# Splitting the experts' weight chunks behind the attention on VectorE alone

## The chip, the cores and the metric

The kernel runs on one core of a Trainium2 chip. The metric is the device time of one execution in microseconds (us); the time before is the median of three runs.

Engines are named as in the profile: PE is TensorE (PEld its weight loads), ACT is ScalarE, DVE is VectorE, POOL is GpSimd, SP is SyncE, which issues most DMAs. Each engine runs its own instructions in the order in which they were written and waits for others by semaphores.

## What is computed

A gated linear attention over 4 x 768 tokens, then two mixture-of-experts layers, each with top-1 routing over 8 experts (model width 384, hidden width 1024). Cut to what matters:

```python
# attention, per batch and head
state = f[t][:, None] * state + outer(k[t], v[t]);  y[t] = q[t] @ state
# each of the two expert layers, on x of [3072, 384]
e = argmax(x @ w_gate);  gate = softmax(x @ w_gate)[e]
out[i] = gate[i] * (relu(x[i] @ w1[e]) @ w2[e])      # w1: 384 x 1024, w2: 1024 x 384
```

The first layer also has a capacity per expert.

## The kernel before

**Stages.** The attention runs over 24 tiles of 128 tokens and ends near 186 us. Then come 19 groups of rows (`G`): 9 of the first expert layer, 10 of the second. A group holds the rows of one expert (256 to 480 of them; an expert with two groups has a row count for each), gathered from DRAM by indirect DMAs that POOL issues (L295), one for each block of up to 128 rows.

**Products in two halves.** Each fp32 operand is held as a high part in the fast fp32r format and a low part, the remainder. A product is three matmuls: high by high, high by low, low by high. So every expert's weights are brought in as 12 raw chunks of 128 x 512 (6 of w1, 6 of w2), and each is split by `_split_chunk`: ACT copies the raw chunk to the high tile (L1025), then a vector engine subtracts it from the raw chunk to give the low tile (L1026). This subtraction, called **the split** below, has two inputs in SBUF and one output there, and nothing else in this kernel is done with it. Which engine takes it is decided at L1063 to L1069.

**A group on PE.** For each of 8 hidden blocks `fc`: `mm1` (L1163, 9 matmuls into a PSUM tile `hp`, of which there are two), on ACT the relu `hh` (L1174), on DVE the low part `hl` (L1175), and two blocks later `mm2` (L1187 to L1189, 9 matmuls). So PE's order is mm1(fc), mm2(fc-2), mm1(fc+1), mm2(fc-1), mm1(fc+2), and mm1(fc+2) needs the `hp` tile that hl(fc) has read last.

**What lies between.** A hand-written plan has 16 spots for a group, two for each fc: one between mm1 and the relu (even spots), one behind mm2 (odd spots). At spots 4 to 9 of the next group a finished group is turned back to rows (PE L926 or L1001, DVE `yr` L927 or L1002, two PSUM tiles shared with the next item); in the first layer also its routing runs there: a chain of small DVE operations (`choose`, L947 and L101 to L125) at spot 6 ends in the one-hot `oh` (L121, L123), which PE's ranking matmul at spot 7 (L131) waits for, then POOL's scatters (L273). In the second layer two small operations (`pw` L996, `td` L997) come ahead of the rows, and POOL scatters the result. At spots 12 and 13 the rows of the next group are turned (PE `tp` L1140, ACT `xh` L1148, DVE `xl` L1149), through the same two PSUM tiles. The 12 splits of the next expert are spread over the spots 0, 1, 2, 4, 5, 6, 8, 9, 10, 12, 13 and 14, and each stands behind what else the plan has at its spot; at an even spot that is ahead of hl on DVE. Single chains stand elsewhere: `flags` (L1287 its last but one) in the fifth group, `first2` with `_skip` (L869) in the eighth.

**The rule for the engine.** During the attention the 12 chunks of the first expert are split on GpSimd by name. Behind it no engine is named (`eng is None`): of the 12 chunks of an expert, those with `i % 3 == 2` went to DVE and the others to POOL, save for the second expert, of which 8 went to DVE and 4 to POOL. Of the 180 chunks behind the attention that makes 64 on DVE and 116 on POOL.

Of the kernel before, what the change touches and what calls it, by code (L numbers as in the profile page):

```python
# [1023 lines left out]
def _split_chunk(nc, hi, lo, raw, eng):  # L1024
    nc.scalar.copy(out=hi, in_=raw)  # L1025
    eng.tensor_tensor(out=lo, in0=raw, in1=hi.bitcast(F32), op=ALU.subtract)  # L1026


class _Weights:
# [23 lines left out]
    def split(self, eng=None):  # L1053
        i = self.done
        wi, c = divmod(i, 2 * NCH)
        k, q = divmod(c, NCH)
        pool = self.env.wp[wi % 2]
        if c == 0:
            self.t[wi] = {}
        if q == 0:  # L1060
            self.t[wi][k] = [
                pool.tile([P, NCC * FF], F32R, name=f"w{k}{u}_{wi}", tag=f"w{k}{u}") for u in "hl"
            ]  # L1063
        hi, lo = self.t[wi][k]
        s = slice(q * RAWC, (q + 1) * RAWC)
        if eng is None:

            eng = self.nc.vector if i % 3 == 2 or wi == 1 and i % 3 else self.nc.gpsimd
        _split_chunk(self.nc, hi[:, s], lo[:, s], self.raws.pop(i), eng)  # L1069
        self.done += 1  # L1070
        self.fetch()

# [729 lines left out]
```

## Time and profile before

| | us |
|---|---|
| median of 3 runs | 707.98 (705.53 to 710.4) |
| the profiled execution | 709.22 |
| its span, first to last instruction | 707.4 |
| PE busy, share of the span | 676.5, 96% |
| DVE busy | 409.8, 58% |
| POOL busy | 361.2, 51% |
| ACT busy | 322.2, 46% |
| mean granted TensorE clock | 0.991 |

An engine's idle time costs something only where PE, which is busy almost throughout, then waits. Ends of matmuls are modelled: a matmul is listed as busy until its result is out, while the next one starts earlier, so an idle time of PE is counted from that later end. "<-" in a row names what ended a wait. A row with "xN" is N instructions merged.

### The profile page before, as it was taken

The page shows a single profiled execution, that of the slowest core. Times are in us where ns is not written, and L with a number is a line of the kernel's source. Part 1 is how long each engine was busy: PE and PEld are TensorE (multiplying, and loading weights), DVE is VectorE, ACT ScalarE, POOL GpSimd, SP SyncE. Part 2 cuts the span into 40 slices and gives each one's busy share as a digit, 9 for nine tenths or more (in the row PEclk, how much of TensorE's full clock was granted, in tenths as well). Part 3 has the DMA queues.
Part 4 walks back from the last instruction along what each step waited for, and adds up shares of the span by engine and source line. Part 5 has one row for each costly group of instructions (what it writes and reads, how often), then busy time and mean ns, then how long its engine had stood idle before and what let it go on. Part 6 is the DMA issues. An engine that isn't in the chain of part 4 may idle for free.

```text
span 707.4 us, 15778 instructions
## 1 busy us (share of the span) xinstructions
PE 676.5 (96%) x5775; PEld 619.0 (87%) x5778; DVE 409.8 (58%) x1024; ACT 322.2 (46%) x697; POOL 361.2 (51%) x389
## 2 busy tenths in 40 slices
PE   7989999989999999999999899989999999999995
PEld 4878788877898989989999899989998899999994
DVE  4767777866486555745546654456344455464641
ACT  5668777743353434344343433144334334354420
POOL 5233444454365546565473651456656464576621
PEclk9999999999999999999999999999999999999998
DMA  8899899532485545355473520275445354454300
GB/s 191 248 203 224 199 183 215 127 83 93 131 258 159 152 120 155 97 154 141 126 185 97 159 95 1 68 237 161 141 115 164 101 155 131 136 154 147 92 25 20
DMA packets 63273, 99.79 MB, mean 141 GB/s; under 512 B 16588, under 2 KB 32942, under 8 KB 63187
## 3 DMA queue, kind: packets, MB, share of 16 engines
q1 hardware_dynamic: 55507, 83.06, 44.0%
q0 software_dynamic: 7680, 15.64, 7.9%
q8 instruction: 47, 0.77, 0.5%
q14 instruction: 39, 0.32, 0.2%
HBM read 82.90 MB, written 16.60 MB: 141 GB/s over the span
## 4 chain that ended last, share of the span: by engine, by line
PE 72%; DVE 9%; DMA 8%; issue 5%; ACT 2%; POOL 1%; SPq 0%; DVEq 0%; POOLq 0%; ACTq 0%
PE hpm L1163 27%; PE ypm L1187 8%; PE ypm L1188 8%; PE ypm L1189 8%; DMA out_dram<-yr,tdm 6%; PE y L509 3%; PE G L402 3%; PE sc L444 3%; PE tpm L1140 2%; PE kv L466 1%; PE tym L926 1%; PE warm L629 1%; PE tym L1001 1%; PE ltm L260 1%; PE kp L433 1%
## 5 line engine op out<-in xcount | busy, mean ns | idle before, releaser
L1174 ACT ACTIVATE hhm<-hpm 128x288 fp32r<-128x288 f32 (+11 forms) x152 | 72.4, 477 | 184.0 <-PE hpm L1163 163.5
L1163 PE MATMUL hpm<-xhm,w0h 128*128 128x288 f32 (+11 forms) x456 | 155.2, 341 | 0.4 <-DVE hlm L1175 0.3
L1187 PE MATMUL ypm<-hhm,w1h 128*128 128x288 f32 (+11 forms) x456 | 153.9, 338 | 0.0
L1175 DVE SCALAR_TENSOR_TENSOR hlm<-hpm,hhm 128x288 fp32r<-128x288 f32 (+11 forms) x152 | 81.2, 536 | 120.9 <-ACT hhm L1174 92.6
L1188 PE MATMUL ypm<-hlm,w1h 128*128 128x288 f32 (+11 forms) x456 | 150.6, 330 | 0.0
L1163 PE MATMUL hpm<-xhm,w0l 128*128 128x288 f32 (+11 forms) x456 | 150.5, 331 | 0.0
L1189 PE MATMUL ypm<-hhm,w1l 128*128 128x288 f32 (+11 forms) x456 | 150.4, 330 | 0.0
L1163 PE MATMUL hpm<-xlm,w0h 128*128 128x288 f32 (+11 forms) x456 | 144.6, 331 | 0.0
L1026 POOL TENSOR_TENSOR w0l<-raw,w0h 128x512 fp32r<-128x512 f32 x64 | 81.9, 1296 | 57.9 <-ACT w0h L1025 57.5
L1026 POOL TENSOR_TENSOR w1l<-raw,w1h 128x512 fp32r<-128x512 f32 x64 | 82.1, 1295 | 41.5 <-ACT w1h L1025 40.6
L295 POOL DMA_INDIRECT xrm<-x,idcm x64 | 69.8, 1090 | 55.6 <-DVE valm L1021 34.0
L1163 PEld LDWEIGHTS hpm<-xhm,w0h 128*128 128x128 f32 x456 | 86.3, 189 | 3.6 <-DVE hlm L1175 1.0
L1187 PEld LDWEIGHTS ypm<-hhm,w1h 128*128 128x128 f32 x456 | 85.9, 188 | 2.8 <-issue 0.6
L1163 PEld LDWEIGHTS hpm<-xhm,w0l 128*128 128x128 f32 x456 | 86.4, 190 | 2.0
L1189 PEld LDWEIGHTS ypm<-hhm,w1l 128*128 128x128 f32 x456 | 85.9, 188 | 2.2
L1188 PEld LDWEIGHTS ypm<-hlm,w1h 128*128 128x128 f32 x456 | 86.0, 189 | 2.1
L1163 PEld LDWEIGHTS hpm<-xlm,w0h 128*128 128x128 f32 x456 | 85.2, 189 | 2.3
L273 POOL DMA_INDIRECT tab<-pos,sum x30 | 30.5, 1018 | 64.8 <-DVE sum L182 58.4
L1148 ACT CAST xhm<-tpm 128x336 fp32r<-128x336 f32 (+8 forms) x64 | 25.2, 435 | 72.1 <-PE tpm L1140 69.0
L1025 ACT CAST w0h<-raw 128x512 fp32r<-128x512 f32 x96 | 57.2, 616 | 0.1
L1025 ACT CAST w1h<-raw 128x512 fp32r<-128x512 f32 x96 | 56.7, 621 | 0.0
L1149 DVE TENSOR_TENSOR xlm<-tpm,xhm 128x336 fp32r<-128x336 f32 (+8 forms) x64 | 29.4, 493 | 42.1 <-ACT xhm L1148 41.2
(209 smaller groups left out, 1040.4 us busy)
## 6 DMA issues: line engine op xcount, KB each, us to landing
raw<-in_w_dram SPq DMA_DIRECT2D x192, 256.0 KB
X<-in_kq_dram SPq DMA_DIRECT2D x48, 192.0 KB
x<-xr SPq DMA_DIRECT2D x8, 582.0 KB
F<-in_fn_dram SPq DMA_DIRECT2D x24, 192.0 KB
Vn<-in_vn_dram SPq DMA_DIRECT2D x24, 192.0 KB
RV<-in_vs_dram SPq DMA_DIRECT2D x48, 48.0 KB
xrm<-x,idcm POOLq DMA_INDIRECT x64
tab<-fill SPq DMA_DIRECT2D x2, 480.0 KB
```

What stands on the lines that cost most here:

```text
L273: ins = tc.nc.gpsimd.indirect_dma_start(out=dst, out_offset=bass.IndirectOffsetOnAxis(ap=idx, axis=0), in_=src, in_offset=None, bounds_che ...
L295: nc.gpsimd.indirect_dma_start(out=dst, out_offset=None, in_=src, in_offset=bass.IndirectOffsetOnAxis(ap=idx, axis=0), bounds_check=bound, ...
L1025: nc.scalar.copy(out=hi, in_=raw)
L1026: eng.tensor_tensor(out=lo, in0=raw, in1=hi.bitcast(F32), op=ALU.subtract)
L1148: nc.scalar.copy(out=g.xh[:, :, s], in_=tp[:, :, :Pr])
L1149: nc.vector.tensor_tensor(out=g.xl[:, :, s], in0=tp[:, :, :Pr], in1=g.xh[:, :, s].bitcast(F32), op=ALU.subtract)
L1163: nc.tensor.matmul(hp[:, :N], w[:, c, fs], x[:, c, :N], start=(k == 0), stop=(k == len(parts) - 1))
L1174: nc.scalar.activation(hh[:, :N], hp[:, :N], AF.Relu)
L1175: nc.vector.scalar_tensor_tensor(out=hl[:, :N], in0=hp[:, :N], scalar=0.0, in1=hh[:, :N].bitcast(F32), op0=ALU.max, op1=ALU.subtract)
L1187: nc.tensor.matmul(g.yp[d][:, :N], w2h[:, fc, ds_], hh[:, :N], start=(fc == 0), stop=False)
L1188: nc.tensor.matmul(g.yp[d][:, :N], w2h[:, fc, ds_], hl[:, :N], start=False, stop=False)
L1189: nc.tensor.matmul(g.yp[d][:, :N], w2l[:, fc, ds_], hh[:, :N], start=False, stop=(fc == NFC - 1))
```

## The change

With no engine named, the split goes to VectorE always. The calls that name an engine (those during the attention) keep it.

```diff
         s = slice(q * RAWC, (q + 1) * RAWC)
-        if eng is None:
-
-            eng = self.nc.vector if i % 3 == 2 or wi == 1 and i % 3 else self.nc.gpsimd
-        _split_chunk(self.nc, hi[:, s], lo[:, s], self.raws.pop(i), eng)
+        _split_chunk(self.nc, hi[:, s], lo[:, s], self.raws.pop(i), eng or self.nc.vector)
         self.done += 1
         self.fetch()
```

The split itself keeps its line, L1026; three lines fewer shift every line number behind L1069 by three (hl is L1172 after the change where it is L1175 before). ACT's copies, their order and the DMAs of the raw chunks stay.

**POOL, around the scatters that follow the routing of the sixth expert's group.** `w0l` and `w1l` are the low tiles, `xrm` gathered rows, `tab` the scatter table. Before:

```order
L295 DMA xrm_7_0_5538<-x_60,idcm_7_0_126 120x388 x2
L1026 TENSOR_TENSOR w0l_5590<-raw_5441,w0h_5589 128x512
L1026 TENSOR_TENSOR w0l_5590<-raw_5458,w0h_5589 128x512
L1026 TENSOR_TENSOR w0l_5590<-raw_5515,w0h_5589 128x512
L1026 TENSOR_TENSOR w0l_5590<-raw_5544,w0h_5589 128x512
L273 DMA tab_63<-pos_74,sum_5_0_5780 30720x4 x4
L1026 TENSOR_TENSOR w1l_5798<-raw_5593,w1h_5797 128x512
L1026 TENSOR_TENSOR w1l_5798<-raw_5610,w1h_5797 128x512
L1026 TENSOR_TENSOR w1l_5798<-raw_5666,w1h_5797 128x512
L1026 TENSOR_TENSOR w1l_5798<-raw_5701,w1h_5797 128x512
```

After:

```order
L273 DMA tab_63<-pos_74,sum_4_0_5420 30720x4 x4
L295 DMA xrm_7_0_5538<-x_60,idcm_7_0_126 120x388 x3
L273 DMA tab_63<-pos_74,sum_5_0_5780 30720x4 x4
L295 DMA xrm_0_0_6005<-x_61,idcm_0_0_129 112x388 x4
L273 DMA tab_63<-pos_74,sum_6_0_6168 30720x4 x3
L273 DMA tab_63<-pos_74,sum_7_0_6428 30720x4 x3
```

Behind the attention POOL has indirect DMAs left and nothing else.

**DVE, spots 4 to 6 of a first-layer group: the turned rows `yr` and the choose chain that ends in `ohm` (L121, L123).** Before:

```order
L927 TENSOR_SCALAR yr_3190<-tym_2_0_0_4540,mtm_2_0_4006 108x384
L1175 SCALAR_TENSOR_TENSOR hlm_3_0_2_4550<-hpm_3_0_2_4524,hhm_3_0_2_4549 128x420
L927 TENSOR_SCALAR yr_3190<-tym_2_0_1_4565,mtm_2_0_4006 108x384
L927 TENSOR_SCALAR yr_3190<-tym_2_0_2_4570,mtm_2_0_4006 108x384
L947 CAST yr_3190<-idxm_2_0_113 108x4
L101 TENSOR_REDUCE lsm_2_0_4595<-rtm_2_0_4575 108x32
L105 TENSOR_REDUCE mxm_2_0_4597<-lsm_2_0_4595 108x4
L109 TENSOR_TENSOR dlm_2_0_4599<-lsm_2_0_4595,mxm_2_0_4597 108x32
L113 SCALAR_TENSOR_TENSOR t1m_2_0_4601<-dlm_2_0_4599,cs 108x32
L117 TENSOR_REDUCE m2m_2_0_4603<-t1m_2_0_4601 108x4
L121 TENSOR_TENSOR ohm_2_0_4605<-cs,m2m_2_0_4603 108x32
L123 TENSOR_TENSOR ohm_2_0_4605<-ohm_2_0_4605,valm_2_0_112 108x32
```

After:

```order
L927 TENSOR_SCALAR yr_3190<-tym_2_0_0_4540,mtm_2_0_4006 108x384
L1026 TENSOR_TENSOR w0l_4471<-raw_4393,w0h_4470 128x512
L1172 SCALAR_TENSOR_TENSOR hlm_3_0_2_4550<-hpm_3_0_2_4524,hhm_3_0_2_4549 128x420
L927 TENSOR_SCALAR yr_3190<-tym_2_0_1_4565,mtm_2_0_4006 108x384
L927 TENSOR_SCALAR yr_3190<-tym_2_0_2_4570,mtm_2_0_4006 108x384
L1026 TENSOR_TENSOR w0l_4471<-raw_4425,w0h_4470 128x512
L947 CAST yr_3190<-idxm_2_0_113 108x4
L101 TENSOR_REDUCE lsm_2_0_4595<-rtm_2_0_4575 108x32
L105 TENSOR_REDUCE mxm_2_0_4597<-lsm_2_0_4595 108x4
L109 TENSOR_TENSOR dlm_2_0_4599<-lsm_2_0_4595,mxm_2_0_4597 108x32
L113 SCALAR_TENSOR_TENSOR t1m_2_0_4601<-dlm_2_0_4599,cs 108x32
L117 TENSOR_REDUCE m2m_2_0_4603<-t1m_2_0_4601 108x4
```

Two splits have come in: one ahead of hl of block 2, one ahead of the choose chain, whose end PE's ranking matmul waits for.

**DVE, spots 12 to 14 of the eighth group: the next group's rows `xlm` and hl of blocks 6 and 7.** Before:

```order
L1146 COPY mtm_7_0_5896<-xrm_7_0_5538 120x6
L1149 TENSOR_TENSOR xlm_7_0_5891<-tpm_7_0_0_5892,xhm_7_0_5890 128x3x120
L1149 TENSOR_TENSOR xlm_7_0_5891<-tpm_7_0_1_5900,xhm_7_0_5890 128x3x120
L1175 SCALAR_TENSOR_TENSOR hlm_6_0_6_5911<-hpm_6_0_6_5880,hhm_6_0_6_5910 128x384
L1149 TENSOR_TENSOR xlm_7_0_5891<-tpm_7_0_2_5923,xhm_7_0_5890 128x3x120
L1026 TENSOR_TENSOR w1l_5798<-raw_5732,w1h_5797 128x512
L1175 SCALAR_TENSOR_TENSOR hlm_6_0_7_5948<-hpm_6_0_7_5933,hhm_6_0_7_5947 128x384
L1175 SCALAR_TENSOR_TENSOR hlm_7_0_0_5977<-hpm_7_0_0_5960,hhm_7_0_0_5976 128x360
```

After:

```order
L1146 TENSOR_TENSOR xlm_7_0_5891<-tpm_7_0_0_5892,xhm_7_0_5890 128x3x120
L1146 TENSOR_TENSOR xlm_7_0_5891<-tpm_7_0_1_5900,xhm_7_0_5890 128x3x120
L1026 TENSOR_TENSOR w1l_5798<-raw_5666,w1h_5797 128x512
L1172 SCALAR_TENSOR_TENSOR hlm_6_0_6_5911<-hpm_6_0_6_5880,hhm_6_0_6_5910 128x384
L1146 TENSOR_TENSOR xlm_7_0_5891<-tpm_7_0_2_5923,xhm_7_0_5890 128x3x120
L1026 TENSOR_TENSOR w1l_5798<-raw_5701,w1h_5797 128x512
L1026 TENSOR_TENSOR w1l_5798<-raw_5732,w1h_5797 128x512
L1172 SCALAR_TENSOR_TENSOR hlm_6_0_7_5948<-hpm_6_0_7_5933,hhm_6_0_7_5947 128x384
L1026 TENSOR_TENSOR w0l_5971<-raw_5865,w0h_5970 128x512
L1172 SCALAR_TENSOR_TENSOR hlm_7_0_0_5977<-hpm_7_0_0_5960,hhm_7_0_0_5976 128x360
```

Each hl here has one or two splits ahead of it; before, only hl of block 7 had one.

## Rows read from the trace of the kernel before

**Rows 1.** The page, busy us of each engine over the span

```profile
PE 676.5 (96%) x5775; PEld 619.0 (87%) x5778; DVE 409.8 (58%) x1024; ACT 322.2 (46%) x697; POOL 361.2 (51%) x389
```

**Rows 2.** Busy time by stretch: engines' busy us, TensorE clock, DMA share, GB/s

```profile
186.00:674.00 488.00, 478.63 (x2934) 450.96 (x2935) 272.51 (x625) 200.71 (x430) 275.69 (x234) 1.00 0.47 138
465.00:484.00 19.00, 17.28 (x129) 16.51 (x128) 13.66 (x27) 8.94 (x20) 12.81 (x11) 1.00 0.64 203
394.90:396.00 1.10, 1.09 (x5) 1.09 (x6) 0.85 (x2) 0.19 (x1) 0.00 (x0) 0.50 0.95 326
396.00:398.00 2.00, 2.00 (x8) 2.00 (x7) 1.20 (x2) 1.30 (x3) 1.13 (x1) 0.52 0.65 237
```

**Rows 3.** PE's waits: line, waited for, us in total, times, longest

```profile
PE tpm L1140 <- DVE xlm L1149: 4.2, 3, 2.6
...
PE tym L1001 <- DVE yr L1002: 2.8, 3, 1.7
...
PE rtm L131 <- DVE ohm L123: 1.4, 2, 0.8
...
PE hpm L1163 <- DVE hlm L1175: 0.3, 1, 0.3
```

**Rows 4.** Timeline of PE at three stops: start us, us, what [idle before]

```profile
391.79 0.34 PE L1188 MATMUL ypm<-hlm,w1h 128*128 128x384 f32 x1
391.97 0.34 PE L1189 MATMUL ypm<-hhm,w1l 128*128 128x384 f32 x1
394.91 0.86 PE L1140 MATMUL tpm<-cs,xrm 120*128 120x120 f32 x3 [2.60 <-DVE xlm L1149]
...
463.27 0.47 PE L1140 MATMUL tpm<-cs,xrm 96*128 96x96 f32 x3 [0.73 <-DVE xlm L1149]
...
698.53 0.53 PE L1001 MATMUL tym<-cs,yTm 128*96 128x128 f32 x3 [0.38 <-DVE yr L1002]
```

**Rows 5.** Timeline of DVE: long operations ahead of PE's stops, one short beside

```profile
296.29 3.25 DVE L1287 SCALAR_TENSOR_TENSOR ff<-ff,badf 128x1 f32<-128x1 f32 x1
...
390.35 0.15 DVE L867 TENSOR_SCALAR lmx<-lmx 128x1 f32<-128x1 f32 x1
390.54 3.06 DVE L869 TENSOR_TENSOR skip<-lmx,p 128x1 f32<-128x1 f32 x1
...
471.07 1.18 DVE L997 TENSOR_TENSOR tdm<-mtm,pwm 112x4 uint32<-112x4 f32 x1
...
653.05 3.31 DVE L1026 TENSOR_TENSOR w0l<-raw,w0h 128x512 fp32r<-128x512 f32 x1 [0.60 <-issue]
```

**Rows 6.** Timeline of POOL at the same times

```profile
296.96 2.55 POOL L1026 TENSOR_TENSOR w1l<-raw,w1h 128x512 fp32r<-128x512 f32 x2
...
389.84 3.74 POOL L1026 TENSOR_TENSOR w1l<-raw,w1h 128x512 fp32r<-128x512 f32 x3
...
653.26 2.54 POOL L1026 TENSOR_TENSOR w0l<-raw,w0h 128x512 fp32r<-128x512 f32 x2
```

**Rows 7.** DVE's splits by shape: busy us, mean ns | idle before, what ended it

```profile
L1026 DVE TENSOR_TENSOR w0l<-raw,w0h 128x512 fp32r<-128x512 f32 x32 | 44.1, 1380 | 12.9 <-ACT w0h L1025 9.0 <-issue 3.9
L1026 DVE TENSOR_TENSOR w1l<-raw,w1h 128x512 fp32r<-128x512 f32 x32 | 34.9, 1097 | 10.9 <-ACT w1h L1025 9.8 <-issue 0.7 <-DMA raw<-in_w_dram 0.5
```

**Rows 8.** The split's line: ns min/median/max, first and last start

```profile
L1026 POOL TENSOR_TENSOR w0l<-raw,w0h x64: 1255/1289/1737, 33.4 to 658.1; 128x512 fp32r<-128x512 f32 x64
...
L1026 DVE TENSOR_TENSOR w0l<-raw,w0h x32: 674/692/3346, 191.3 to 661.3; 128x512 fp32r<-128x512 f32 x32
L1026 DVE TENSOR_TENSOR w1l<-raw,w1h x32: 676/693/3732, 203.1 to 673.1; 128x512 fp32r<-128x512 f32 x32
```

**Rows 9.** Timeline at a ranking: DVE's one-hot, PE's matmul on it

```profile
319.99 0.19 DVE L123 TENSOR_TENSOR ohm<-ohm,valm 105x32 bf16<-105x32 bf16 x1
...
321.56 0.18 PE L131 MATMUL rtm<-ohm,trib 105*105 105x32 bf16 x1
```

**Rows 10.** Timeline: a split on DVE inside an indirect DMA's issue on POOL

```profile
309.00 0.69 DVE L1026 TENSOR_TENSOR w0l<-raw,w0h 128x512 fp32r<-128x512 f32 x1 [0.51 <-ACT w0h L1025]
...
308.78 1.03 POOL L295 DMA_INDIRECT xrm<-x,idcm  x1 [0.30 <-issue]
```

## The prediction

> **What bounds the kernel now.** I read the page's busy times first: PE is busy in 96% of the span, and no other engine is above 58% [rows 1]. So only what PE waits for counts. The table by stretch narrows that to the part where the change acts, from 186 us (the end of the attention) to 674 us (the last split): PE is busy for 478.63 of 488.00 us there, so 9.4 us is all the idle time there is [rows 2]. The waits by line give it names: PE waits for DVE's xl (4.2 us, 3 times), yr (2.8, 3 times), one-hot (1.4, twice) and hl (0.3, once) [rows 3]. No wait for weights and none for POOL is among them.
>
> Then DVE's timeline just ahead of each stop, beside POOL's. The longest stop of PE, 2.60 us [rows 4], follows an operation on one column, `skip`, of 3.06 us; its neighbour of the same size takes 0.15 us [rows 5]. POOL ran three splits merged from 389.84 to 393.58, and `skip` ended at 393.60 [rows 5, 6]. `ff` is the same: 296.29 to 299.54 beside POOL's two splits to 299.51. The split on DVE at 653.05 took 3.31 us and ended 0.56 us behind POOL's two, which end at 655.80. `td` at 471.07 stood 1.18 us. So a DVE operation that reads two SBUF operands waits until POOL's run of splits is over, and the PE stops behind DVE are late echoes of that.
>
> **The change, part by part.**
>
> *Removed from POOL:* 116 splits of 1.289 us (the median) [rows 8], 149.5 us. POOL ends nothing on PE's path, so this itself is worth nothing.
>
> *Added to DVE:* 116 splits. One that nothing holds up takes 0.692 us (the median [rows 8]): 80.3 us. The 64 that DVE has now cost 44.1 + 34.9 = 79.0 us [rows 7], where 64 x 0.692 would be 44.3: 34.7 us of them is waiting for POOL. With no split on POOL this goes, so DVE's splits grow from 79.0 to 180 x 0.692 = 124.6 us, by 45.6 us, and DVE from 272.5 of 488 us [rows 2] to about 318 (less the held-up ff, skip and td), some 65%. Free time on DVE pays for all of this, as long as no single stretch runs short.
>
> *The tightest stretch* is the 288-row group from 465 to 484 us, whose 16 spots take all 12 splits: DVE is busy for 13.66 of 19.00 us [rows 2]. In it four splits stand on DVE now; by the mean of the first row of [rows 7], 1.380, they hold 5.5 us, and td about 1 us too much. That leaves 7.2 for the rest, and 12 x 0.692 makes 15.5. The stretch also has PE stops of some 1.7 us in it (19.00 - 17.28), and if they go it is 17.3 long: 90% full. A DVE split also waits for ACT's copy: (9.0 + 9.8)/64 = 0.3 us on average [rows 7]. Were all 12 waits idle time that nothing else fills, 3.6 us more, 19.1 would stand against 17.3. Bounds for this place: 0 (these waits fall into time in which DVE would idle anyway) to 1.8 us.
>
> *Where an added split stands ahead of work that PE waits for:* (a) hl. PE's order leaves three blocks of 9 matmuls between mm1(fc) and the reuse of its PSUM tile. At 288 rows a block lasts 1.2 us (my estimate: the 384-row matmuls of [rows 4] start 0.18 us apart, so 9 x 0.18 x 288/384), so hl has 3.6 us. It has at most 480 columns, fewer than a split's 512, so I estimate it under 0.7 us; one or two splits ahead of it add 0.7 or 1.4. The trace has tried worse: DVE splits were up to 3.35 and 3.73 us long [rows 8], most with an hl next behind them, and PE waited for hl once in the whole run, 0.3 us [rows 3]. Cost 0. (b) The choose chain at spot 6 has one split more directly ahead of it and one two items earlier. In the row shown the one-hot was ready at 319.99 + 0.19 = 320.18 and PE came for it at 321.56 [rows 9]: 1.38 us to spare, against 0.69, or 1.38 if neither is absorbed. Cost from below 0 (where the chain was held up it now comes earlier) to some 0.4 us for a narrower group with less to spare, over seven such groups at most 2.8 us. I take 0.5 us for (b) and the tight stretch together, near the low end, since the row shown covers the one certain split twice.
>
> *What comes back on PE.* From [rows 3] I take off the two waits with another cause: 0.73 us at 463.27, where xl waits for its high half and no split is near, and 0.38 us at 698.53, behind the last split [rows 4]. Left are (4.2 - 0.7) + (2.8 - 0.4) + 1.4 + 0.3 = **7.6 us** in 7 stops. Idle time is counted from a modelled end: the matmuls at 391.79 and 391.97 are 0.18 us apart but listed as 0.34 long [rows 4], so each stop hides 0.16 us more, 7 x 0.16 = **1.1 us**. And behind the longest stop, in which PE stood from 392.3 to 394.9, the granted clock was 0.50 and then 0.52, the 1.2 GHz level instead of 2.4, until 398.0: of 3.1 us, 1.10 x 0.50 + 2.00 x 0.52 = 1.6 were worth full speed [rows 2], **1.5 us** lost. Together 10.2 us.
>
> [...] DVE will hold 180 splits against the indirect DMAs that stay on POOL. A split at 309.00 that ran wholly inside the issue of one (308.78 to 309.81) took 0.69 us [rows 10], as long as any. [...]
>
> *Sum.* The profiled execution: 709.22 - 10.2 + 0.5 = 699.5 us (its span 707.4 becomes 697.7). The median of the three runs shown is 1.2 us lower than the profiled execution, so I forecast **698.3 us**.
>
> **The rivals.**
>
> *A, forecast:* the stops behind DVE go, hardly anything comes in their place: 698.3, its own range 694.5 to 701.
>
> *B, within 1%: the added splits take more than half of it back.* If the choose chain is late by 0.4 us in seven groups (2.8), the tight stretch by 1.8, and the clock still falls once (1.5), 6.1 us instead of 0.5 is given back: 708.0 - 10.2 + 6.1 = 703.9. For it: one-hot and rows are exactly what PE waits for now. Against: most of those waits have a held-up operation ahead of them. The stretch in which it decides is the narrowest group that has a choose chain, when its spare time is under 0.69 us.
>
> *C, slower: DVE becomes what PE waits for.* Fourteen experts have two places where two splits adjoin ahead of an hl (spots 0 to 2 and 12 to 14). Were hl late by one split at each, 14 x 2 x 0.69 = 19.3 us, and 708.0 - 10.2 + 19.3 = 717. It decides from where DVE has no free time: in the 465 us stretch at (17.3 - 7.2)/12 = 0.84 us a split, waits included; over the whole part at (488 - 272.5 + 79.0)/180 = 1.6 us. At 0.69 + 0.3 the first is passed (the 1.8 us above) and the second far away, and [rows 3, 8] show splits of over 3 us that PE did not notice.
>
> [...]
>
> *E, nothing changes:* the waits of [rows 3] would have to come from ACT or a DMA. Against: ff and skip end with POOL's splits to 0.03 us. Some 707.
>
> **How the numbers follow.** A 0.66, B 0.20, C 0.05, D 0.05, E 0.04. 1% of 707.98 is 7.1 us, about what a measurement of this kernel can tell from no change; the three runs shown lie 4.9 us apart. Faster by over 1% means under 700.9: most of A, not its upper edge, 0.60. Slower means over 715.1: C, 0.05. Within 1%: 0.35. The range takes in A, B and D: 694.5 (all of the 10.2, and the spread of the runs) to 705.0. It leaves out C and E and the tails, 2 in 10.
>
> **What would show each step right or wrong.** In the profile of the changed kernel: (1) no split on POOL behind the attention, POOL's busy time near 361 - 150 = 212 us; (2) 180 splits on DVE with a median and a maximum near 0.69 us, where the maximum is now 3.73; were it 1.5, D holds; (3) ff, skip and td at 0.15 to 0.2 us; (4) PE's waits for xl down to 0.7 us, for yr to 0.4, none or little for the one-hot; a wait for the one-hot that has grown is B, one for hl is C; (5) full clock from 391 to 398 us; (6) the first 186 us as before. Wrong I am if PE stops as often as now with DVE busy at 90% in front of each stop, or if the stops go and the span still doesn't get shorter: then PE's own rate was the bound and the idle time no loss.

## The result and the profile after

The changed kernel takes **698.52 us** (median of 4 runs, 696.49 to 699.27) against 708.77 for the kernel before, run beside it (4 runs, 705.53 to 710.4): ratio 0.9852, 95% interval 0.9821 to 0.9884. That is faster by 1.5%, and 0.2 us from the forecast of 698.3. The four runs lie 2.8 us apart. The profiled execution took 698.58 us, with a span of 696.8 where the kernel before has 707.4.

The page of the changed kernel, busy us (as [rows 1]):

```profile
PE 673.1 (97%) x5778; PEld 618.9 (89%) x5778; DVE 431.6 (62%) x1140; ACT 322.5 (46%) x697; POOL 223.1 (32%) x273
```

Its busy time by stretch (columns as [rows 2]): the part behind the attention, its tightest stretch, and the matmuls that follow the rows of the ninth group, which were granted 0.50 and 0.52 of the clock before the change [rows 2]:

```profile
186.00:664.00 478.00, 477.13 (x2941) 451.77 (x2941) 290.25 (x741) 200.51 (x430) 137.09 (x118) 1.00 0.48 139
465.00:480.00 15.00, 15.00 (x117) 15.00 (x116) 10.97 (x30) 7.27 (x18) 7.08 (x6) 1.00 0.71 217
...
389.80:392.00 2.20, 2.20 (x14) 2.20 (x14) 2.20 (x4) 1.76 (x4) 0.00 (x0) 1.00 0.86 270
```

PE is idle for 0.87 of 478 us now, where it was idle for 9.4 of 488. Its waits from 186 us to the end (as [rows 3]) are the two for DVE that the prediction had set aside:

```profile
PE tpm L1137 <- DVE xlm L1146: 0.7, 1, 0.7
PE tym L1001 <- DVE yr L1002: 0.4, 1, 0.4
```

Where PE stood for 2.60 us [rows 4], its timeline runs through:

```profile
388.59 0.34 PE L1186 MATMUL ypm<-hhm,w1l 128*128 128x384 f32 x1
388.77 0.47 PE L1137 MATMUL tpm<-cs,xrm 120*128 120x120 f32 x3
```

The operations that were long [rows 5], by source line (ns min/median/max, first and last start):

```profile
L1284 DVE SCALAR_TENSOR_TENSOR ff<-ff,badf x1: 160/160/160, 294.4 to 294.4; 128x1 f32<-128x1 f32 x1
...
L869 DVE TENSOR_TENSOR skip<-lmx,p x1: 161/161/161, 387.2 to 387.2; 128x1 f32<-128x1 f32 x1
...
L997 DVE TENSOR_TENSOR tdm<-mtm,pwm x10: 157/163/164, 461.2 to 685.2; 96x3 uint32<-96x3 f32 x4, 112x4 uint32<-112x4 f32 x2, 120x4 uint32<-120x4 f32 x1, 104x4 uint32<-104x4 f32 x1
```

And the split's line (as [rows 8]):

```profile
L1026 DVE TENSOR_TENSOR w0l<-raw,w0h x90: 676/684/698, 188.6 to 649.8; 128x512 fp32r<-128x512 f32 x90
L1026 DVE TENSOR_TENSOR w1l<-raw,w1h x90: 676/685/764, 199.0 to 661.3; 128x512 fp32r<-128x512 f32 x90
```

**Where the time went.** The same matmul stands in both traces, so its two start times tell how far ahead the changed kernel is there. From PE's timelines, us:

| matmul behind ... | before | after | ahead by | since the row above |
|---|---|---|---|---|
| the attention (L1160) | 189.14 | 188.12 | 1.02 | 1.02 |
| the first one-hot, hl (L1160) | 200.81 | 198.43 | 2.38 | 1.36 |
| the matmul `pk` (L1423) | 294.48 | 292.37 | 2.11 | -0.27 |
| ff, xl (L1160) | 305.90 | 302.51 | 3.39 | 1.28 |
| skip, xl and the half clock (L1160) | 397.82 | 390.31 | 7.51 | 4.12 |
| the one-hot at 414.8 (L131) | 414.81 | 406.51 | 8.30 | 0.79 |
| td, yr (L1001) | 473.35 | 463.01 | 10.34 | 2.04 |
| yr, xl (L1001) | 494.72 | 484.00 | 10.72 | 0.38 |
| the split of 3.31 us, yr (L1001) | 659.98 | 648.06 | 11.92 | 1.20 |
| last matmul into ypm (L1186) | 696.72 | 684.75 | 11.97 | 0.05 |
| end of the span | 707.4 | 696.8 | 10.6 | -1.3 |

Behind the attention 10.95 us are gained, most of it at the stops. 1.0 us more stands ahead of 189 us, and 1.3 us is lost behind the last matmul; no split that the change moves stands in either place.

The 1.0 us is what is left of two larger differences. At 184 us the changed kernel is 3.5 us ahead; 1.5 us of that come between 150 and 160 us, where the kernel before was granted half the clock for a while (0.50 from 153 to 155 us) and the changed one all of it (1.00). The kernel with the other experts (next section), which runs the same instructions as the kernel before up to there, is 3.5 us ahead as well, so no moved split makes this difference. The stretch before, then after:

```profile
150.00:156.00 6.00, 4.32 (x63) 3.63 (x57) 3.20 (x7) 2.44 (x7) 4.59 (x7) 0.72 0.37 68
150.00:156.00 6.00, 4.27 (x85) 3.42 (x82) 3.96 (x9) 3.00 (x7) 4.58 (x7) 1.00 0.37 66
```

By 189 us the changed kernel has lost 2.5 us of its lead again, to a wait of 1.69 us for gathered rows and to a clock of 0.50 behind it (shown below, where it is run again).

### The profile page after: what moved, and what is told of

It is laid out like the page before. It is cut to its first block, busy times and chain, and to the rows that moved or that the text cites. A ratio compares the mean times of both kernels' runs of the same rounds, so it can differ in the third digit from the quotient of the medians.

```text
span 696.8 us, 15753 instructions
## 1 busy us (share of the span) xinstructions
PE 673.1 (97%) x5778; PEld 618.9 (89%) x5778; DVE 431.6 (62%) x1140; ACT 322.5 (46%) x697; POOL 223.1 (32%) x273
## 4 chain that ended last, share of the span: by engine, by line
PE 84%; DVE 6%; issue 3%; POOL 2%; DMA 2%; ACT 2%; POOLq 0%; DVEq 0%
PE hpm L1160 31%; PE ypm L1184 11%; PE ypm L1185 11%; PE ypm L1186 11%; PE sc L444 3%; PE G L402 3%; PE y L509 3%; PE tpm L1137 3%; PE tym L1001 2%; PE tym L926 2%; PE kv L466 1%; PE kp L433 1%; PE ltm L260 1%; DVE QT L422 1%; POOL tab L273 1%
## 5 line engine op out<-in xcount | busy, mean ns | idle before, releaser
L1160 PE MATMUL hpm<-xhm,w0h 128*128 128x288 f32 (+11 forms) x456 | 154.7, 340 | 0.0
L1186 PE MATMUL ypm<-hhm,w1l 128*128 128x288 f32 (+11 forms) x456 | 150.9, 331 | 0.0
L1160 PE MATMUL hpm<-xhm,w0l 128*128 128x288 f32 (+11 forms) x456 | 150.4, 331 | 0.0
L1172 DVE SCALAR_TENSOR_TENSOR hlm<-hpm,hhm 128x288 fp32r<-128x288 f32 (+11 forms) x152 | 81.4, 536 | 105.9 <-ACT hhm L1171 103.6
L1160 PE MATMUL hpm<-xlm,w0h 128*128 128x288 f32 (+11 forms) x456 | 144.2, 330 | 0.0
L295 POOL DMA_INDIRECT xrm<-x,idcm x64 | 71.5, 1117 | 138.3 <-PE hpm L1160 50.6
L1160 PEld LDWEIGHTS hpm<-xhm,w0h 128*128 128x128 f32 x456 | 86.2, 189 | 2.7 <-issue 0.2
L1186 PEld LDWEIGHTS ypm<-hhm,w1l 128*128 128x128 f32 x456 | 86.2, 189 | 2.2
L1160 PEld LDWEIGHTS hpm<-xhm,w0l 128*128 128x128 f32 x456 | 86.3, 189 | 2.0
L1160 PEld LDWEIGHTS hpm<-xlm,w0h 128*128 128x128 f32 x456 | 84.9, 188 | 2.3
L273 POOL DMA_INDIRECT tab<-pos,sum x30 | 33.1, 1105 | 142.3 <-DVE sum L182 135.9
L273 POOL DMA_INDIRECT out_dram<-yr,tdm x34 | 42.4, 1247 | 89.6 <-DVE yr L1002 83.5
L1026 DVE TENSOR_TENSOR w0l<-raw,w0h 128x512 fp32r<-128x512 f32 x90 | 60.1, 686 | 9.4 <-ACT w0h L1025 8.9
L1026 DVE TENSOR_TENSOR w1l<-raw,w1h 128x512 fp32r<-128x512 f32 x90 | 59.7, 688 | 0.3
```

Source lines behind the costliest of these rows:

```text
L273: ins = tc.nc.gpsimd.indirect_dma_start(out=dst, out_offset=bass.IndirectOffsetOnAxis(ap=idx, axis=0), in_=src, in_offset=None, bounds_che ...
L295: nc.gpsimd.indirect_dma_start(out=dst, out_offset=None, in_=src, in_offset=bass.IndirectOffsetOnAxis(ap=idx, axis=0), bounds_check=bound, ...
L1160: nc.tensor.matmul(hp[:, :N], w[:, c, fs], x[:, c, :N], start=(k == 0), stop=(k == len(parts) - 1))
L1172: nc.vector.scalar_tensor_tensor(out=hl[:, :N], in0=hp[:, :N], scalar=0.0, in1=hh[:, :N].bitcast(F32), op0=ALU.max, op1=ALU.subtract)
L1186: nc.tensor.matmul(g.yp[d][:, :N], w2l[:, fc, ds_], hh[:, :N], start=False, stop=(fc == NFC - 1))
```

## The experiments

Each varies the lines of `split` that choose the engine, from the kernel before or the changed one; the code shows the lines that matter, shortened. The theory is the prediction's: DVE work beside a run of splits on POOL is held until the run is over, and only where PE meets such an echo does it cost time. Its rivals: every split on POOL costs its share; POOL's work as such costs, or its place in the queue; DVE has little room. Times are medians; a ratio is to the kernel before, run beside it.

**Six experts, and the others.** The chunks that were split ahead of PE's stops belong to six experts. The first kernel moves those alone to DVE (44 of the 116 splits), the second all others (72).

```diff
+            old = (self.nc.vector if i % 3 == 2 or wi == 1 and i % 3 else self.nc.gpsimd)
+            eng = self.nc.vector if wi in (1, 4, 7, 8, 9, 15) else old    # first
+            eng = old if wi in (1, 4, 7, 8, 9, 15) else self.nc.vector    # second
```

> 44 of the 116 splits go to VectorE: those of the six experts (the 2nd, 5th, 8th, 9th, 10th and 16th set of weights) whose splits run while PE stops at 198.9, 300, 392, 414, 471 and 659 us of the kernel before. The other 72 stay on GpSimd. Theory 1 (a split on GpSimd holds up VectorE operations with two inputs in SBUF, and only the six places where PE then stops cost time): nearly all of the gain, 698.5 to 700.5 us. Theory 2 (the gain follows the number of splits moved, since a split takes 0.69 us on VectorE and 1.29 on GpSimd): 44/116 of 10.2 us, so 704.9 us.

> The complement: the 72 splits of the other nine experts go to VectorE, the 44 of the six experts stay as they were. Theory 1: the six stops stay, 706.5 to 709 us. Theory 2: 72/116 of 10.2 us, so 702.4 us.

The first took 698.97 us (695.88 to 699.08; ratio 0.9864, 0.9818 to 0.9909), as theory 1 has it: with 72 splits still on POOL it is as fast as the changed kernel, and from 190 us to the last ypm matmul the two traces take the same time to 0.5 us. Its splits by source line, and PE's waits from 186 us on:

```profile
L1026 DVE TENSOR_TENSOR w0l<-raw,w0h x54: 676/692/3682, 187.8 to 650.2; 128x512 fp32r<-128x512 f32 x54
```

```profile
PE tpm L1140 <- DVE xlm L1149: 0.7, 1, 0.7
PE tym L1001 <- DVE yr L1002: 0.4, 1, 0.4
```

A split of 3.68 us is there, and PE doesn't notice it. The second took 704.07 us (702.37 to 707.25; ratio 0.9963, 0.9941 to 0.9986), 5.6 us behind the changed kernel as first measured. The stop at skip stands, and behind the one at td the clock falls; the last ypm matmul comes at 691.85 us, 7.1 later than in the changed kernel. PE's timeline, then the stretches behind the two stops:

```profile
391.53 0.53 PE L1140 MATMUL tpm<-cs,xrm 120*128 120x120 f32 x3 [2.30 <-DVE xlm L1149]
```

```profile
391.50:393.50 2.00, 1.97 (x13) 1.98 (x14) 1.41 (x3) 1.41 (x3) 0.35 (x1) 1.00 0.97 319
...
470.00:472.00 2.00, 2.00 (x10) 2.00 (x10) 0.88 (x2) 0.81 (x2) 1.70 (x2) 0.50 0.45 110
```

By the first kernel it is the few places, not the number of splits. The second doesn't settle it by its time: 704.07 lies outside both forecasts (706.5 to 709, and 702.4). Its trace shows where it is faster than theory 1 had it. Its span is 5.9 us shorter than that of the kernel before (701.5 against 707.4): 3.0 us stand ahead of 196 us, where both still run the same instructions; 1.6 at skip, behind which the clock stays full this time; 1.2 where the stop at 660 us was, since `pw` started 0.04 us ahead of POOL's split this time and took 0.15 us instead of 1.03, so that only td was held; 1.0 behind the last ypm matmul (9.68 us there against 10.70, see below). 1.2 us are lost to the half clock behind td.

**What on POOL holds DVE.** All splits stay on DVE as after the change, and for each of the 116 chunks that it split before POOL does other work on the raw chunk, whose result nobody uses: a subtraction as long as a split, or three memsets.

```diff
+            self.nc.gpsimd.tensor_tensor(out=raw, in0=raw, in1=hi[:, s].bitcast(F32), op=ALU.subtract)   # reads
+            for _ in range(3): self.nc.gpsimd.memset(raw, 0.0)                                           # writes only
```

> The changed kernel with 116 operations put back on GpSimd, for the chunks that it split before: a subtraction of the same shape with the same two inputs, written over the raw chunk, which nobody reads any more; it runs behind VectorE's split of the same chunk. The product is the same. Theory 1: VectorE is held up again, operations of 2 to 3 us come back and with them some of the stops: 702 to 710 us. Theory 2: nothing is undone, 698.5 us. Theory 3 (what cost time was GpSimd's queue: gathers and scatters were issued late behind its splits): 706 to 709 us.

> As the run with the shadow subtractions, but GpSimd writes zeros over the raw chunk instead, three times 512 columns for each of the 116 chunks, some 1.4 us, and reads nothing. Same waits, same place in GpSimd's queue, about the same busy time. Theory 1: VectorE's second read is left alone, 698 to 700 us, and no split on VectorE over 0.8 us. Theory 3: 706 to 709 us, as the queue is as full as before.

The subtractions: 702.82 us (701.29 to 704.88; ratio 0.9921, 0.9901 to 0.9942), in theory 1's range. The memsets: 694.63 us (693.5 to 696.15; ratio 0.9811, 0.9771 to 0.9851), below every range named; 2.3 us of that is a shorter end of the program (9.69 us behind the last ypm matmul, see below), and up to that matmul its trace is level with the changed kernel's (0.1 us). DVE's timeline and POOL's with the subtractions:

```profile
390.61 2.95 DVE L871 SCALAR_TENSOR_TENSOR cum<-lsel,skip,cum 128x8 bf16<-128x8 f32 x1
```

```profile
391.01 2.52 POOL L1069 TENSOR_TENSOR raw<-raw,w1h 128x512 f32<-128x512 f32 x2
```

`skip` itself was 0.16 us this time; the operation two behind it met POOL's run and ended with it (393.56 against 393.53), and PE stood 2.21 us at the same place. With the memsets, POOL's group (busy us, mean ns) and the splits by source line:

```profile
L1070 POOL MEMSET raw<- 128x512 f32 x348 | 181.8, 529 | 65.8 <-DVE w0l L1026 44.2 <-DVE w1l L1026 8.2
```

```profile
L1026 DVE TENSOR_TENSOR w0l<-raw,w0h x90: 676/686/698, 188.3 to 649.7; 128x512 fp32r<-128x512 f32 x90
L1026 DVE TENSOR_TENSOR w1l<-raw,w1h x90: 678/686/751, 198.7 to 661.2; 128x512 fp32r<-128x512 f32 x90
```

There are 182 us of POOL work here, more than the 149.5 us that the change removed, and no split of DVE takes over 0.751 us (0.764 in the changed kernel). So what holds the splits is neither POOL's time nor its queue. Beside the subtractions, which read SBUF, they took up to 2.64 us, beside the memsets, which only write it, at most 0.751. Small operations with a single input in SBUF are another matter: `pw` took 0.61 us beside the memsets and ended with one (619.79 against 619.77).

**How much room DVE has.** Each of the 180 splits done twice on DVE:

```diff
+            self.nc.vector.tensor_tensor(out=lo[:, s], in0=raw, in1=hi[:, s].bitcast(F32), op=ALU.subtract)
```

> The changed kernel, but behind the attention VectorE does each of the 180 splits twice, one right behind the other, with the same result: every split now takes some 1.38 us of VectorE instead of 0.69, and GpSimd has none. Theory 1 (VectorE has room until a split costs more than the spare time of the tightest stretch, which the prediction put at 0.84 us a split from 465 to 484 us): the loss stands in that stretch, where VectorE is busy for 10.97 of 15.00 us after the change and would get 12 x 0.69 = 8.3 us more, so about 4 to 6 us, and little elsewhere: 702 to 706 us. Theory 2 (the prediction's case C: every split that stands ahead of hl or of the choose chain makes TensorE wait by its length): 28 places x 0.69 = 19 us and more, 717 us or above, with stops of TensorE for hl in every group. Theory 3 (VectorE isn't near any bound): 698 to 699 us.

It took 722.28 us (721.87 to 723.57; ratio 1.0184, 1.0153 to 1.0215): theory 2's price. PE's waits from 186 us on, then the tightest stretch and two others by engine:

```profile
PE tpm L1140 <- DVE xlm L1149: 4.2, 3, 2.2
PE rtm L131 <- DVE ohm L123: 3.9, 6, 1.5
PE pk L1426 <- DVE okb L1424: 3.2, 1, 3.2
PE hpm L1163 <- DVE hlm L1175: 2.6, 4, 1.0
...
PE tym L1001 <- DVE yr L1002: 0.9, 2, 0.5
PE hpm L1163 <- DVE w0l L1069: 0.4, 1, 0.4
```

```profile
485.00:503.00 18.00, 16.25 (x121) 15.54 (x120) 17.48 (x41) 7.48 (x17) 6.27 (x7) 1.00 0.56 168
203.00:206.00 3.00, 3.00 (x15) 3.00 (x16) 2.79 (x13) 0.63 (x2) 0.00 (x0) 0.56 0.56 167
303.00:309.00 6.00, 6.00 (x18) 5.71 (x19) 3.57 (x14) 0.00 (x0) 1.66 (x2) 0.50 0.51 154
```

The tight stretch is full (17.48 of 18.00) and costs 3.3 us: the matmul at 459.52 us of the changed kernel is 19.7 us late here, the one at 478.54 23.0. Theory 1 had this place, at 4 to 6 us. The rest stands at places that it called uncritical: the choose chain, hl, and the matmul `pk` in the fifth group, which waits for DVE's `okb`; and in the clock of 0.56 and 0.50 behind them. The waits sum to 15.2 us against 1.1 in the changed kernel; 15 more stops hide 0.16 us each (2.4), and the two half-clock stretches lose 3.0 x 0.44 + 6.0 x 0.50 = 4.3. Together that is 14.1 + 2.4 + 4.3 = 20.8. It fits: the changed kernel's matmul at 189.96 us comes 1.8 us later here, the one at 646.22 23.3 us, 21.5 more. PE waits for hl four times, not 28: theory 2's price, not its mechanism.

**The opposite: all 180 on GpSimd.**

```diff
-        _split_chunk(self.nc, hi[:, s], lo[:, s], self.raws.pop(i), eng or self.nc.vector)
+        _split_chunk(self.nc, hi[:, s], lo[:, s], self.raws.pop(i), eng or self.nc.gpsimd)
```

> The opposite rule: behind the attention all 180 splits on GpSimd, none on VectorE. GpSimd's busy time grows by 64 x 1.29 = 83 us over before, to about 444 us. Theory 1 (what costs is a VectorE operation that stands behind GpSimd's runs of splits, whatever that operation is): the runs get longer, skip, ff and td are held as before or for longer, and TensorE stops for xl, yr and the one-hot at least as in the kernel before: 708 to 716 us. Theory 2 (what costs is VectorE's own splits, which are held and hold what is queued behind them; with no splits on VectorE it has time to spare): the stops get fewer, 699 to 704 us.

It took 731.22 us (727.62 to 733.2; ratio 1.0292, 1.0246 to 1.0338). The direction is theory 1's, the size is beyond it. DVE's timeline and POOL's:

```profile
644.03 5.51 DVE L996 TENSOR_SCALAR pwm<-valm 104x4 f32<-104x4 f32 x1
```

```profile
642.02 7.48 POOL L1026 TENSOR_TENSOR w0l<-raw,w0h 128x512 fp32r<-128x512 f32 x6
```

POOL's runs are up to six splits long, and `pw`, four columns, ends with the run (649.54 against 649.50). DVE has no split behind the attention here and is the less busy for it (374.4 us), and PE waits for xl 11.0 us, for yr 6.8, for hl 2.9. In four stretches behind its stops the clock is at half, 17.1 us together, so up to 8.5 us are lost to that; the mean granted clock is 0.98 from 186 to 697 us, where the changed kernel has 1.00 from 186 to 664. Of the operations that theory 1 named, ff is held (4.29 us), skip isn't (0.16). `pw` has a single SBUF input beside a constant: it isn't only operations with two that are held.

**The attention's splits on DVE too.**

```diff
+        _split_chunk(self.nc, hi[:, s], lo[:, s], self.raws.pop(i), self.nc.vector)
```

> The changed kernel with the 12 splits during the attention on VectorE as well, so that GpSimd does none at all. Theory 1 (a GpSimd split costs only where it makes a VectorE operation late that TensorE waits for, and during the attention these 12 do so hardly at all): 697 to 699.5 us with the part up to 186 us unchanged within 1 us. Theory 2 (each GpSimd split costs by itself): 12 x 10.7 / 116 = 1.1 us faster in the part up to 186 us. Apart from both, the end of the program: the time from the last matmul into ypm to the end was 12.0 us in the changed kernel and 9.7 us in three of its relatives, with GpSimd's next instruction behind its last taken branch 2.8 against 0.4 us later. If that goes by where the branch lies in GpSimd's program (here some 24 instructions earlier), this kernel may show either end.

It took 698.39 us (696.81 to 699.05; ratio 0.9844, 0.9815 to 0.9874). The time is theory 1's, but it doesn't tell the two apart: at 190 us this trace is 3.2 us ahead of the changed kernel's, not within 1 us, and the second execution of the changed kernel (next) is 2.6 us ahead there with no edit at all. PE waited for a one-hot (1.0 us) and an hl (0.3) once more, though POOL has no split at all: in the group ahead of it DVE's `yr` started at 192.20 us after 1.47 us of idle time, which the profile puts down to a matmul into `hp`, a tile that `yr` doesn't read. So a stop at this place can have another cause, which stays open. The end of the program was the long one, 11.84 us.

**One stop by itself, and the changed kernel again.** Of the 116 splits only the 8 of the eighth expert go back to POOL.

```diff
+            eng = self.nc.gpsimd if wi == 7 and i % 3 != 2 else self.nc.vector
```

> The changed kernel once more, beside the next three: 698 to 699 us, the time from the last matmul into ypm to the end again near 12.0 us, with GpSimd's next instruction 2.8 us behind its last taken branch.

> The changed kernel, but the 8 chunks of the eighth expert that were on GpSimd before are there again (8 of 116); they are the ones behind which skip took 3.06 us and TensorE's longest stop followed. Theory 1 (the terms of the prediction's sum for this stop: 2.6 us of waiting, 0.16 hidden by the modelled end, 1.5 for the granted clock behind it): 4.3 us more than the changed kernel beside it, 702.8 us; skip again 2.5 to 3.1 us, the granted clock at half level for some 3 us behind the stop. Theory 2 (each split on GpSimd costs the same share): 10.7 x 8 / 116 = 0.7 us more, 699.2. Theory 3 (the stop alone counts, without a loss by the clock): 2.8 us more, 701.3.

The changed kernel: 697.17 us (695.53 to 699.53; ratio 0.9862, 0.9828 to 0.9896), under the 698 to 699 expected; its end is 12.13 us, as expected. With the 8 splits: 701.75 us (700.42 to 703.09; ratio 0.9919, 0.9891 to 0.9947), 4.6 us more, and 3.2 more than the first measurement of the changed kernel. Of the kernel with the 8 splits, DVE's timeline, PE's, and the stretch behind the stop:

```profile
388.23 3.06 DVE L869 TENSOR_TENSOR skip<-lmx,p 128x1 f32<-128x1 f32 x1
```

```profile
392.30 0.53 PE L1139 MATMUL tpm<-cs,xrm 120*128 120x120 f32 x3 [2.31 <-DVE xlm L1148]
```

```profile
393.40:395.50 2.10, 2.10 (x14) 2.10 (x13) 1.59 (x2) 1.96 (x4) 1.30 (x1) 1.00 0.75 260
```

`skip` is 3.06 us to the digit [rows 5], and the stop is back, but the clock behind it is full. In the trace the stop costs 2.4 us (ahead of it this kernel is 1.1 us behind the changed one's first trace, behind it 3.5). That is nearest to theory 3's 2.8, while by the medians the cost lies at theory 1's 4.3. The other differences between these traces stand ahead of 190 us, and two executions of the changed kernel alone show how they come about. The stretch there, the first execution's, then the second's:

```profile
185.20:187.70 2.50, 2.50 (x14) 2.50 (x13) 1.54 (x3) 0.85 (x2) 0.00 (x0) 0.50 1.03 389
```

```profile
184.00:186.50 2.50, 2.50 (x24) 2.50 (x23) 1.66 (x4) 1.73 (x5) 0.00 (x0) 1.00 0.95 304
```

In the first, PE waited 1.69 us for gathered rows at 184.86 us and then ran at a clock of 0.50, 14 matmuls in the time of 24; in the second it waited 0.46 and 0.94 and kept 1.00. At 184 us the second is 1.15 us ahead, at 189 us 2.6, and it stays so to the last matmul. The stop at the rows of the ninth group left the clock full here (2.31 us), with the other experts (2.30) and with the subtractions (2.21), and halved it in the kernel before (2.60) and with all splits on GpSimd (4.74; the nine matmuls behind it took 2.89 us there, 1.66 with the other experts). How often it falls there in the kernel before, one trace of it can't say; so it stays open which of the two theories the medians speak for.

**The end of the program.** In the kernels so far, the time from the last ypm matmul to the end of the span was 9.7 us in three (the other experts, subtractions, memsets), 10.7 in the kernel before and with all splits on GpSimd, and 11.8 to 12.0 in four (the changed kernel, six experts, splits done twice, the attention's too). In three of the last four, what follows POOL's last branch (it jumps over a block that isn't needed) comes 2.7 to 2.8 us after it, not 0.5; in the fourth, the attention's, the next instruction comes after 0.5 us and the gap, 2.2 us, stands two instructions further on. To shift that place in POOL's program, POOL gets one-column memsets of a tile of its own, one behind each of the first 72 (or 12) splits:

```diff
+        if eng is None and i < 2 * NCH + 72:
+            self.nc.gpsimd.memset(self.env.pad, 0.0)
```

> The changed kernel with 72 memsets of one column of a tile of its own on GpSimd, one behind each of the first 72 splits behind the attention; nothing reads that tile. It asks about the end of the program, not about the splits. Theory 1 (how late GpSimd's first instruction behind its last taken branch comes goes by the branch's place in its program; with 72 instructions more it lies as in the relatives with the short end): the end shrinks from 12.0 to 9.7 us, nothing else moves, 696.2 us. Theory 2 (it goes by how much GpSimd has done, or differs from run to run): the end stays at 12.0 us and the time at 698.5 us, or slower if the memsets get into the way of the indirect DMAs.

> The changed kernel with 12 memsets of one column on GpSimd behind the first 12 splits behind the attention, a control to the one with 72. Where GpSimd's last taken branch had 539 to 699 of its instructions in the trace ahead of it in three kernels with the long end (539, 555, 699) and 627, 647, 763, 785, 913 and 995 in those with the short one, this one has about 567. Theory 1 (the place of the branch decides): the long end as in the changed kernel, 11.9 to 12.0 us from the last matmul into ypm, and 698.5 us. Theory 2 (any memsets on GpSimd shorten the end): 9.7 us and 696.2 us.

> The kernel with 72 memsets once more, beside the changed kernel on the same chip, to see whether it is the faster one of the two. Theory 1 (the end is 2.3 us shorter and nothing else differs): 2.0 to 2.6 us faster than the changed kernel beside it, about 696. Theory 2 (the difference of the medians of other runs was chance): the same time as the changed kernel.

With 72: 696.14 us (693.82 to 699.11; ratio 0.9813, 0.9769 to 0.9857) and, the second time, 694.50 (691.94 to 694.66; ratio 0.9810, 0.9778 to 0.9842). With 12: 695.17 us (694.41 to 698.36; ratio 0.9840, 0.9806 to 0.9875). By source line, POOL's last branch and the semaphore instructions behind it (ns min/median/max, then the us of the first and the last start), of the changed kernel, with 12 and with 72 memsets:

```profile
L1665 POOLq EVENT_SEMAPHORE  x4: 17/30/43, 691.2 to 691.5; - x4
...
L1665 POOLq COMPARE_BRANCH  x1: 53/53/53, 688.4 to 688.4; - x1
```

```profile
L1668 POOLq EVENT_SEMAPHORE  x4: 17/30/43, 687.8 to 688.1; - x4
...
L1668 POOLq COMPARE_BRANCH  x1: 53/53/53, 685.0 to 685.0; - x1
```

```profile
L1668 POOLq EVENT_SEMAPHORE  x4: 17/30/43, 687.2 to 687.5; - x4
...
L1668 POOLq COMPARE_BRANCH  x1: 45/45/45, 686.7 to 686.7; - x1
```

From the branch to what follows it are 2.8, 2.8 and 0.5 us; the ends are 12.02, 11.98 and 9.68 us. So 12 memsets do nothing to the end and 72 shorten it: theory 1 of both, as far as the end goes. That it is the place in the program that counts, and not something else about the 60 further memsets, is argued from this and not shown. For the time the end isn't enough: with 12 memsets the kernel undercut theory 2's 696.2 although its end was long (its runs overlap with those of the changed kernel), and with 72 it was 2.7 us faster than the changed kernel beside it, a little more than the 2.0 to 2.6 expected. All three runs with the small memsets have PE run a little faster over a long part: from the matmul at 381.56 us of the changed kernel to the one at 613.22 it takes 231.66 us, with 12 memsets 230.40 (379.60 to 610.00), in the second execution of the changed kernel as much as in the first. The kernel with the 348 large memsets takes 231.65 there, so it isn't memsets on POOL as such. What sets the three apart is the added tile with its memsets; it may shift the addresses of others, but that was not tried.

The kernel with 72 memsets is faster than the changed one: its six times of the last comparison end (694.66) below the lowest of the changed kernel (695.53). The kernel with the 348 large memsets is as fast (694.63, in another comparison). Neither is a remedy to copy: what 72 of them gain is mostly the shorter end, which, if the argument above holds, hangs on how many instructions happen to stand ahead of it.

## Why the prediction was right

**The bound, and where its time was.** The 9.4 us of PE's idle time were the right place to look: PE's idle time is 0.87 us now. With the six experts whose splits stood ahead of the stops, the whole gain is there; the 72 other splits add nothing to it beyond 0.5 us. The list of waits left out one row, PE's wait for gathered rows, whose DMAs POOL issues; 0.73 us of it lie inside the 9.4:

```profile
PE tpm L1140 <- DMA xrm<-x,idcm: 1.3, 2, 0.7
```

No split stands there and no term of the sum used it, but it is the place at which the changed kernel's first trace lost 2.5 us.

**The sum.** 7.6 + 1.1 + 1.5 - 0.5 = 9.7 us were forecast behind the attention, 10.95 came. By the starts of the same matmuls the seven stops gave back 8.7 us, as much as the 7.6 + 1.1 forecast, and the half clock behind skip 1.4 where 1.5 stood. The two frequencies that the prediction names beside the 1.5 are in no trace: the profile gives the clock as a share of full speed, 0.50 and 0.52 there [rows 2]. Of the half us for the choose chain and the tight stretch only 0.27 us was asked for, and elsewhere: at the matmul `pk`, where `okb` came later. The rest, some 1.2 us, comes in steps of under 0.3 us that the sum had no term for, two of them at gaps of PE too short for the list of waits.

**The hit on 0.2 us is partly luck.** The 1.0 us ahead of 189 us and the end's -1.3 us were in no term and cancelled, and the 1.0 us is itself 3.5 less 2.5. Two executions of the changed kernel lie 2.6 us apart at 189 us alone, and its second measurement, 697.17, is 1.1 us from the forecast.

**Step by step.** The prediction's first sign was right but for a size: POOL has no split behind the attention, but it is busy for 223.1 us, not 212. Its indirect DMAs have grown; the groups of the kernel before, then of the one after (busy us, mean ns):

```profile
L295 POOL DMA_INDIRECT xrm<-x,idcm x64 | 69.8, 1090 | 55.6 <-DVE valm L1021 34.0 <-issue 13.9 <-PE tpm L1140 6.1
L273 POOL DMA_INDIRECT out_dram<-yr,tdm x34 | 36.6, 1076 | 33.6 <-DVE yr L1002 27.1 <-issue 5.6 <-DVE hlm L1175 0.6
L273 POOL DMA_INDIRECT tab<-pos,sum x30 | 30.5, 1018 | 64.8 <-DVE sum L182 58.4 <-issue 5.2 <-PE hpm L1163 0.6
```

```profile
L295 POOL DMA_INDIRECT xrm<-x,idcm x64 | 71.5, 1117 | 138.3 <-PE hpm L1160 50.6 <-issue 46.3 <-PE tpm L1137 22.3
L273 POOL DMA_INDIRECT out_dram<-yr,tdm x34 | 42.4, 1247 | 89.6 <-DVE yr L1002 83.5 <-issue 3.4 <-DVE hlm L1172 1.5
L273 POOL DMA_INDIRECT tab<-pos,sum x30 | 33.1, 1105 | 142.3 <-DVE sum L182 135.9 <-issue 5.5 <-DVE mtm L1143 0.6
```

That is 1.7 + 5.8 + 2.6 = 10.1 of the 11 us. Four signs came as forecast: (2) the 180 splits have a median of 0.684 to 0.685 us, the longest takes 0.764; (3) ff, skip and td take 0.16; (4) PE waits 0.7 us for xl, 0.4 for yr and not at all for the one-hot; (5) the clock is full behind skip. The last did not: (6) the first 186 us are not as before, but 3.5 us shorter by 184 us, as they are with the other experts, whose program is that of the kernel before up to there.

**The rivals.** B's price for the choose chain didn't come in the changed kernel at 0.69 us a split; at twice that it did, 3.9 us in six waits, so the chain's spare time lies between. (The one wait of 1.0 us with the attention's splits on DVE has a late `yr` ahead of it.) C's price comes with twice the splits, by other places than its own, and sooner: the prediction's 1.6 us a split over the whole part is no threshold, since 1.38 us already cost 21.5 us. D, 0.05 of the chances, was that indirect DMAs hold up the splits, and the 1.5 us that the second sign gives it are shown by no run: no split took over 0.764 us, and it is the indirect DMAs that take longer beside the splits, up to 2.43 us against 1.12 (last section). E, that nothing changes, is out by the six experts.

**What was too narrow.** "A DVE operation that reads two SBUF operands" is held; `pw`, with one, stood 5.51 us. It doesn't always wait until POOL's run of splits is over, either: ahead of the stop at td POOL ran four splits from 466.77 to 472.23 us, and DVE's split of 468.36 us ended at 469.85 and `pw` at 471.03, inside the run; only td ended with it. And the 1.5 us for the clock were read from one execution: a stop of 2.31 us at the same place left it full.

## What to carry to other kernels

When the engine that sets the time waits for VectorE, look at what VectorE does just ahead of the stop: a one-column operation of 3 us that ends with a GpSimd instruction names the cause (`skip`, 3.06 us, took 0.16 without one), and moving the GpSimd work that reads SBUF away from those few places was worth as much here as moving all of it (698.97 us against 698.52). A split that is shorter on the busier engine (0.69 us on VectorE, 1.29 on GpSimd) can still be cheaper there, as long as the chains that end in a wait of the bound have more to spare than the work put ahead of them; once they haven't, as with 1.38 us a split, the wait comes, and the half clock behind it can cost as much again (3.2 and 3.0 us at `pk`). A hit within 0.2 us proves little where two terms that nobody forecast cancel: compare the start of the same matmul in both traces.

## What was not expected of the hardware

**VectorE's splits lengthen POOL's issue of the indirect DMAs beside them.** POOL's timeline of the changed kernel, then DVE's:

```profile
624.11 2.43 POOL L273 DMA_INDIRECT out_dram<-yr,tdm  x1 [0.30 <-DVE yr L1002]
626.84 1.00 POOL L273 DMA_INDIRECT out_dram<-yr,tdm  x1 [0.30 <-DVE w1l L1026]
```

```profile
624.35 1.28 DVE L1026 TENSOR_TENSOR w0l<-raw,w0h 128x512 fp32r<-128x512 f32 x2
...
626.12 0.69 DVE L1026 TENSOR_TENSOR w1l<-raw,w1h 128x512 fp32r<-128x512 f32 x1
```

The first took 2.43 us around two splits and the start of a third, the second 1.00 us just behind that. Of the changed kernel's 124 indirect DMAs behind the attention, the 58 without a split beside them took at most 1.12 us each on POOL, the 66 others up to 2.43; with all splits on GpSimd none of the 124 took over 1.12. It cost PE nothing: from 190 us on PE's list of waits has none for a DMA.

**At the end of GpSimd's program some kernels stand still for over 2 us.** Behind its last branch the next instruction came after 2.7 to 2.9 us with 555, 567, 571 and 699 of the engine's instructions in the trace ahead of the branch, and after 0.5 with 627, 647, 763, 785, 913 and 995. With 539 it came after 0.5 us too, and the gap stood two instructions further on. So it seems to go by the place in the program and not by the branch as such. Why it does, no run here shows.

**The clock's fall doesn't go by the stop's length alone.** The granted clock fell to 0.50 at PE's stops of 2.60 us [rows 2], 1.73 (at td, with the other experts' splits moved) and 1.69 (184.86 us), and stayed at 1.00 at those of 2.31, 2.30 and 2.21 us ahead of the ninth group. At td itself the kernel before stopped for 1.72 us and kept 1.00.
